# A fourth block pair in 11 products instead of 12, with the order of a pair's work searched anew

## The chip, the cores and the metric

The kernel runs on one core of a Trainium2 chip. The metric is the device time of one execution in microseconds (us). The engines are named as in the profile: PE multiplies matrices, DVE, ACT and POOL work on elements, SP issues most transfers.

## The reference

Input x has 8 sequences of 4096 tokens of 192 channels. A causal convolution of 7 taps (softmax weights, one set for each of 8 heads of 24 channels) is followed by an RMS norm and a gated layer with 1536 inner columns, all in float32:

```python
x_pad = np.concatenate([np.zeros((B, 6, D)), x], axis=1)        # 6 rows of zeros ahead of each sequence
y = np.einsum('hk,bskhg->bshg', w, windows_of_7(x_pad))          # w: softmax over the 7 taps
xn = y / np.sqrt(np.mean(y * y, axis=-1) + 1e-6) * rms_g
g, val = xn @ w_gate, xn @ w_val                                 # 192 -> 1536, twice
out = (g / (1 + np.exp(-g)) * val) @ w_out                       # 1536 -> 192
```

## The kernel before, in words

**Tiles.** The 32768 tokens are cut into 32 "pairs" of two tiles of 512 tokens. Pair 0 and pair 1 run in plain forms while the weights are prepared. Pairs 2 to 31, thirty of them, run the same program, and make nearly all of the time. The 1536 inner columns are cut into six "block pairs" j = 0 to 5 of 2 x 128 columns. A block pair has four cells: a, b, c, d, for two token tiles times two column blocks. A cell fills one two-bank PSUM tile (gate in one bank, value in the other), and there are four such tiles (`duo`). The upper 64 rows of PE work on the value, the lower 64 on the gate.

**Gate products.** The 192 input channels are three chunks of 64. In the plain form a cell is the sum of three products (letters A, B, E), 12 for a block pair. In the other form two of the chunks are multiplied as 2 x 2 blocks with seven products instead of eight (Strassen-Winograd), and the third chunk takes four: 11 products, P1 to P7 and Q1 to Q4. FORM says which block pair takes which form. A product is 6 matmuls (L898: three split parts, gate and value). In the 11-product form cells share sums, and this needs work on PSUM between products of one block pair:

- f1 copies cell a to b after P1 (ACT, L666), and P6 then adds into b;
- f3 copies cell c after P5 to SBUF (ACT at L666, or DVE at L668);
- f4 writes c = b + that copy (DVE, L969) after P6; P7 then adds into b;
- f5 writes d = b + that copy (DVE, L969) after P7, into the PSUM tile that cell a has given back; only then may the next product write on in b (Q3 or P4) or d (Q4).

When a cell is complete, `Ag` (ACT, L975) takes the silu of the gate, and `Vm` (DVE, L982) multiplies it by the value into `ht`; `Vm` gives the PSUM tile back. So a cell's tile is free for a later product only after silu and multiply.

**Output steps.** The output product uses seven products for 2 x 2 blocks too: seven forms o1 to o7 times six blocks, 42 steps of 6 small matmuls (L925; 12 records in the trace). Four "h" sums for each block (h1 to h4, DVE or POOL, L952) make their inputs. The three accumulators X, Y, Z sit in PSUM tiles; C22 and C21 (DVE, L999) and the copies c1, c2, s7 (ACT) collect them, and T11, T12, T21, T22 (DVE transposes, L940) turn them for the store (L1031).

**Token side.** For the next pair ahead: `cv0` to `cv6` are the convolution's taps (L432, L436), then square, reduce, `pow`, `bc`, `mul` make the norm; `pl` writes it to a scratch array and `ft` reads it back transposed (`xb`); x1 to x4 (L826) are the sums of token blocks for the 11-product form; n, l, d (L666, L812, L814) split the five operands into three float32r parts; `ld` loads the rows of x of the pair after that (`xh`).

**Order.** Every engine runs its instructions in the order in which they are issued. That order is written by hand or search in strings: LINE is the order of PE's 69 products and 42 steps of one pair; ORDER interleaves everything else with it. In ORDER, `p3` is the next three entries of LINE; a word's first letter is the engine (V DVE, A ACT, G POOL, S SP); `-` means the pair before, `+` the pair after. So `p5-` are five of the previous pair's output steps. FIRST is the same for pair 1, with W for the next step of the preparation of weight pieces. SP keeps a ring of ten weight pieces (192 KB each) filled: a piece's slot is loaded anew, in the order of first use, when its last product has been issued (`ring_load`, L784).

**Weight pieces.** `prepare` makes ten kinds of pieces (o = 0 to 9) for the block pairs that use them, splits them in three parts and writes them to the array `wd` (L748 to L767). `blocks` picks the block pairs: a slice with a constant step where the set has one, or else all six.

**Padding rows.** The first pair of each sequence has six rows of zeros ahead; `load_head` clears them in `xh` (L150).

Of the kernel before, what the change touches and what calls it, by code (L numbers as in the profile page):

```python
# [20 lines left out]
def kernel(  # L21
# [10 lines left out]
    nc = tc.nc  # L32
# [3 lines left out]
    H, K = weight.shape  # L36
    GS = D // H
# [9 lines left out]
    HALO = K - 1  # L47
# [20 lines left out]
    SPAN = 1509  # L68
    SPLIT = 2.0**-12
    HIGH = 0xFFFFF000  # L70
    FORM = (1, 0, 1, 0, 1, 0)
    PLAIN = tuple((j, c) for j in range(NP) for c in "abcd")
    ORDER = (
# [14 lines left out]
    )  # L88
    FIRST = (
# [12 lines left out]
    )  # L102
    LINE = (
# [7 lines left out]
    )  # L111

    cst = ctx.enter_context(tc.tile_pool(name="cst", bufs=1))
# [9 lines left out]
    x0 = cst.tile([P, NJ + HALO, D], F32, name="x0")  # L123
# [3 lines left out]
    def queue(eng):  # L127
        return nc.scalar if eng == "A" else nc.sync
# [8 lines left out]
    def load_head(p, b, t0, h, eng="S"):  # L137

        t = x_sb[p]

        def get(dst, tb, h, dims, r):
            row = x[b, t0 + tb * TB + r - HALO, h * GS :]
            src = bass.AP(
                tensor=row.tensor, offset=row.offset, ap=[dims, [D, TB + HALO - r], [1, GS]]
            )
            queue(eng).dma_start(out=dst, in_=src)  # L146

        first = int(t0 == 0)
        if first and h == 0:
            nc.gpsimd.memset(t[0:H, 0:HALO, :], 0.0)  # L150
            get(t[0:H, HALO:, :], 0, 0, [GS, H], HALO)
        get(t[first * H + h :: H], first, h, [TB * D, P // H - first], 0)

# [6 lines left out]
    def load(p):  # L160
# [34 lines left out]
        out=ps[6][:, 0 : H * K], lhsT=ones[:], rhs=w_row[:], start=True, stop=True,  # L195
# [24 lines left out]
    def load_in(u, q):  # L220
# [18 lines left out]
    nw = 4 * NP * (D // 2)  # L239
    tw = x0[:].rearrange("p j d -> p (j d)")[:, 0:nw].rearrange(  # L240
        "p (i k d) -> p i k d", i=4, k=NP
    )
    hs = work.tile([P, NP, T], F32, name="hs")
    tt = work.tile([P, 9, T], F32, name="tt")
    tiles = [tt[:, i, :] for i in range(few)]
# [2 lines left out]
    def load_out(i):  # L248
# [22 lines left out]
        out=taps[:], in0=w_sb, in1=stat[:].to_broadcast([P, H, K]), op=ALU.subtract  # L271
# [7 lines left out]
        out=taps[:], in0=taps[:], in1=ssum[:].to_broadcast([P, H, K]), op=ALU.mult  # L279
# [101 lines left out]
    def conv_first(mine, share):  # L381

        t = x_sb.pop(0)
        y = ys[0] = yp.tile([P, NJ, D], F32, name="y")
        theirs = [k for k in range(K) if k not in mine]
        two = NJ // 4
        for i, k in enumerate([theirs[0], mine[-1]] + theirs[1:]):
            xk, m = t[:, k : k + NJ, :], next(kept)
            cuts = (0, share) if k in mine else (0, H // 2, H)
            if k == theirs[-1]:  # L390
                cuts = (0, H // 2, H // 2 + 2, H)
            for lo, hi in zip(cuts, cuts[1:]):
                for h in range(lo, hi):
                    hs = slice(h * GS, (h + 1) * GS)
                    nc.scalar.mul(m[:, :, hs], xk[:, :, hs], taps[:, h, k : k + 1])
                part = slice(lo * GS, hi * GS)
                for c in range(4):
                    to = ps[c][:, 0 : two * D].rearrange("p (j d) -> p j d", d=D)
                    nc.tensor.matmul(
                        out=to[:, :, part], lhsT=unity, rhs=m[:, c * two : (c + 1) * two, part],  # L400
                        start=(i == 0 and lo == 0), stop=True, skip_group_check=True,
                    )
        for k in mine:
            xk = t[:, k : k + NJ, :]
            for h in range(share if k == mine[-1] else 0, H):
                hs = slice(h * GS, (h + 1) * GS)
                w = taps[:, h, k : k + 1]
                if k == mine[0]:
                    nc.vector.tensor_scalar(
                        out=y[:, :, hs], in0=xk[:, :, hs], scalar1=w, scalar2=None, op0=ALU.mult  # L410
                    )
                else:
                    nc.vector.scalar_tensor_tensor(
                        out=y[:, :, hs], in0=xk[:, :, hs], scalar=w, in1=y[:, :, hs],
                        op0=ALU.mult, op1=ALU.add,
                    )
        for c in range(4):
            at = y[:, c * two : (c + 1) * two, :].rearrange("p j d -> p (j d)")
            nc.vector.tensor_tensor(out=at, in0=ps[c][:, 0 : two * D], in1=at, op=ALU.add)
            if c % 2:  # L420
                heat(at, c)
# [296 lines left out]
    def blocks(o):  # L718

        kind = {2: 1, 4: 1, 6: 1, 8: 1, 9: 0}.get(o)  # L720
        mine = [j for j in range(NP) if kind in (None, FORM[j])]
        step = {b - a for a, b in zip(mine, mine[1:])}
# [419 lines left out]
    def done(it):  # L1142
# [21 lines left out]
        out=mask[:], in_=unity.rearrange("p (i h) -> p h i", h=H), axis=AX.X, op=ALU.add  # L1164
    )
    nc.vector.tensor_tensor(
        out=own[:], in0=taps[:].rearrange("p h k -> p k h"),
# [5 lines left out]
    load_out(1)  # L1173
    load_in(1, nc.sync)
    conv_first((1, 3, 5, 6), 2)
    nc.sync.dma_start(out=rg_sb[LOW, :], in_=rg)
    nc.sync.dma_start(out=rg_sb[UPP, 0 : KP - 1], in_=rg[:, 1:KP])
    nc.sync.dma_start(out=rg_sb[UPP, KP - 1 : KP], in_=rg[:, 0:1])
# [6 lines left out]
    p, sl, v = plain(first_hts)  # L1185
# [95 lines left out]
```

## Time and profile before

| what | us |
|---|---|
| three runs, median (range) | 2492.14 (2491.06 to 2493.56) |
| the profiled execution, its own time | 2491.27 |
| its span (first to last instruction) | 2489.5 |
| PE busy | 2475.4 |
| DVE busy | 2014.9 |
| ACT busy | 926.5 |
| POOL busy | 847.1 |
| matmuls at L898 (gate products) | 12420 |
| matmul records at L925 (output steps) | 16200 |

The granted PE clock is full speed from end to end. The transfer queue that carries all the kernel's own data is busy for 63.6% of the 16 engines' span. One line of the timeline view has the start, the duration, the engine, the source line and operation, output and inputs, shapes and the count of instructions merged in it; in brackets stands the idle time before it, and what ended that.

### The profile page before, as it was taken

The page shows a single profiled execution, that of the slowest core. Times are in us where ns is not written, and L with a number is a line of the kernel's source. Part 1 is how long each engine was busy: PE and PEld are TensorE (multiplying, and loading weights), DVE is VectorE, ACT ScalarE, POOL GpSimd, SP SyncE. Part 2 cuts the span into 40 slices and gives each one's busy share as a digit, 9 for nine tenths or more (in the row PEclk, how much of TensorE's full clock was granted, in tenths as well). Part 3 has the DMA queues.
Part 4 walks back from the last instruction along what each step waited for, and adds up shares of the span by engine and source line. Part 5 has one row for each costly group of instructions (what it writes and reads, how often), then busy time and mean ns, then how long its engine had stood idle before and what let it go on. Part 6 is the DMA issues. An engine that isn't in the chain of part 4 may idle for free.

```text
span 2489.5 us, 69349 instructions
## 1 busy us (share of the span) xinstructions
PE 2475.4 (99%) x29332; PEld 1971.8 (79%) x29332; DVE 2014.9 (81%) x2492; ACT 926.5 (37%) x1345; POOL 847.1 (34%) x634
## 2 busy tenths in 40 slices
PE   8999999999999999999999999999999999999999
PEld 5547778888788887888887788887888788888787
DVE  8678878888878788878788787888787888888874
ACT  6443333333334333334333343333333333333331
POOL 0542333323343324243333333233433243433331
PEclk9999999999999999999999999999999999999999
DMA  7365667766667666667666677666676666776652
GB/s 150 60 197 152 162 160 190 182 176 157 157 171 201 172 168 159 161 176 200 170 158 156 166 194 178 177 157 157 171 205 170 164 161 157 183 196 174 152 148 80
DMA packets 702935, 412.23 MB, mean 166 GB/s; under 512 B 508834, under 2 KB 688930, under 8 KB 702626
## 3 DMA queue, kind: packets, MB, share of 16 engines
q1 hardware_dynamic: 698880, 406.89, 63.6%
q8 instruction: 231, 3.78, 0.7%
q10 hardware_dynamic: 3746, 0.92, 0.2%
q14 instruction: 78, 0.64, 0.1%
HBM read 349.26 MB, written 58.39 MB: 164 GB/s over the span
## 4 chain that ended last, share of the span: by engine, by line
PE 95%; DMA 2%; DVE 1%; SPq 1%; issue 1%; POOL 0%; ACT 0%; DVEq 0%; POOLq 0%; ACTq 0%
PE ps L898 57%; PE ps L925 36%; PE ps L870 2%; DMA xb<-xd 1%; DVE ht L1097 0%; SPq L146 0%; SPq L230 0%; DVE y L436 0%; DMA hs<-in_moe_w_out_dram 0%; DMA x<-in_x_dram 0%; DMA ht<-in_moe_w_gate_dram 0%; DMA ht<-in_moe_w_val_dram 0%; DVE part L336 0%; POOL part L327 0%; DVE part L321 0%
## 5 line engine op out<-in xcount | busy, mean ns | idle before, releaser
L898 PE MATMUL ps<-part,ring 64*128 64x512 f32 x12420 | 1443.4, 389 | 0.0
L898 PEld LDWEIGHTS ps<-part,ring 64*128 64x128 f32 x12420 | 1234.7, 184 | 188.1 <-issue 18.3
L975 ACT ACTIVATE tt<-ps 128x512 f32<-128x512 f32 x744 | 431.8, 598 | 759.4 <-PE ps L898 719.7
L982 DVE TENSOR_TENSOR ht<-ps,tt 128x512 f32<-128x512 f32 x744 | 495.8, 685 | 190.0 <-ACT tt L975 184.9
L925 PE MATMUL ps<-ht,wo_sb 128*32 128x384 f32 (+2 forms) x7272 | 474.7, 380 | 1.9 <-DVE ht L982 1.0
L925 PE MATMUL ps<-ht,x 128*32 128x256 f32 (+2 forms) x6696 | 441.9, 379 | 0.0
L952 POOL TENSOR_TENSOR ht<-ht 128x512 f32<-128x512 f32 x183 | 280.0, 1544 | 431.3 <-PE ps L925 377.2
L925 PEld LDWEIGHTS ps<-ht,wo_sb 128*32 128x32 f32 x7272 | 320.1, 110 | 128.7 <-issue 23.1
L952 POOL TENSOR_TENSOR hs<-ht 128x512 f32<-128x512 f32 x90 | 116.4, 1294 | 835.9 <-DVE ht L982 833.6
L925 PEld LDWEIGHTS ps<-ht,x 128*32 128x32 f32 x6696 | 302.5, 110 | 90.7
L436 DVE SCALAR_TENSOR_TENSOR y<-xh,tp,y 128x1536 f32<-128x1536 f32 x186 | 342.8, 1843 | 1.3
L666 ACT COPY ps<-ps 128x384 f32<-128x384 f32 (+1 forms) x121 | 104.1, 860 | 409.6 <-PE ps L898 312.9
L969 DVE TENSOR_TENSOR ps<-ps,tt 128x1024 f32<-128x1024 f32 x180 | 221.3, 1229 | 42.6 <-PE ps L898 35.6
L666 ACT COPY tt<-ps 128x384 f32<-128x384 f32 (+1 forms) x122 | 90.9, 745 | 227.1 <-PE ps L925 207.9
L925 PE MATMUL ps<-hs,x 128*32 128x128 f32 (+2 forms) x2232 | 161.0, 379 | 0.0
L925 PEld LDWEIGHTS ps<-hs,x 128*32 128x32 f32 x2232 | 108.8, 110 | 27.8
L952 DVE TENSOR_TENSOR ht<-ht 128x512 f32<-128x512 f32 x189 | 127.4, 688 | 3.4 <-PE ps L925 3.3
L666 ACT CAST part<-xb 128x1024 fp32r<-128x1024 f32 x87 | 91.4, 1050 | 89.5 <-PE ps L898 75.9
L952 DVE TENSOR_TENSOR ht<-hs,ht 128x512 f32<-128x512 f32 x155 | 121.2, 798 | 2.9 <-PE ps L925 1.1
L952 DVE TENSOR_TENSOR hs<-ht 128x512 f32<-128x512 f32 x96 | 121.8, 1269 | 2.1
L814 DVE SCALAR_TENSOR_TENSOR part<-part,xb 128x1024 fp32r<-128x1024 f32 x87 | 106.2, 1221 | 0.0
L812 DVE TENSOR_TENSOR part<-xb,part 128x1024 fp32r<-128x1024 f32 x87 | 105.5, 1213 | 0.0
(132 smaller groups left out, 1389.7 us busy)
## 6 DMA issues: line engine op xcount, KB each, us to landing
ring<-wd SPq DMA_DIRECT2D x1350, 192.0 KB
xb<-xd SPq DMA_DIRECT2D x60, 512.0 KB
xd<-xh SPq DMA_DIRECT2D x240, 96.0 KB
xh<-in_x_dram SPq DMA_DIRECT2D x192, 105.0 KB
xb<-xd SPq DMA_DIRECT2D x60, 256.0 KB
out_dram<-o_sb SPq DMA_DIRECT2D x126, 96.0 KB
out_dram<-o_sb SPq DMA_DIRECT2D x62, 128.0 KB
wd<-part SPq DMA_DIRECT2D x5, 1152.0 KB
```

Source lines behind the costliest of these rows:

```text
L436: nc.vector.scalar_tensor_tensor(out=y, in0=xk, scalar=w, in1=y, op0=ALU.mult, op1=ALU.add)
L666: nc.scalar.copy(out=dst, in_=src)
L812: e.tensor_tensor(out=split_of(g, 1).bitcast(F32R), in0=src, in1=high, op=ALU.subtract)
L814: nc.vector.scalar_tensor_tensor(out=split_of(g, 2).bitcast(F32R), in0=high, scalar=1.0 + SPLIT, in1=src, op0=ALU.mult, op1=ALU.subtract,)
L870: nc.tensor.matmul(out=self.both(j, c)[:, h, :], lhsT=wf[HALF[h], k, 2 * j + f, :], rhs=rb[HALF[h], k, g, :], start=(k == 0), stop=(k == K ...
L898: nc.tensor.matmul(out=self.both(j, c)[:, h, :], lhsT=left[HALF[h]], rhs=right[HALF[h]], start=(first and q == 0), stop=True, skip_group_c ...
L925: nc.tensor.matmul(out=self.acc(b)[i * Q : (i + 1) * Q, at : at + n], lhsT=left, rhs=cols, start=fresh, stop=True, skip_group_check=True, ...
L952: engine[eng].tensor_tensor(out=dst, in0=a, in1=b, op=op)
L969: nc.vector.tensor_tensor(out=self.both(j, c), in0=self.both(j, "b"), in1=s5, op=ALU.add)
L975: nc.scalar.activation(out=tt[:, t, :], in_=self.both(j, c)[:, 0, :], func=AF.Silu)
L982: nc.vector.tensor_tensor(out=self.hv(j, "abcd".index(c)), in0=self.both(j, c)[:, 1, :], in1=tt[:, t, :], op=ALU.mult,)
```

## The change

FORM becomes (0, 1, 1, 0, 1, 1): block pairs 1, 2, 4, 5 in 11 products (block pairs 0, 2, 4 before), so LINE has 68 products and 42 steps. ORDER, FIRST and LINE are other sequences. With four block pairs 1, 2, 4, 5 there is no constant step, so `blocks` returns all six for the pieces 2, 4, 6, 8 (three before), and two (0 and 3) for piece 9. In ORDER the token sums x1 to x4 and the splits l are all on DVE (POOL had x2, x3, x4 and one l), and the four f1 are on ACT, three f3 on ACT and one on DVE. In `load_head` the zeros come by a transfer from a small tile that POOL clears once, instead of a POOL memset each time.

```diff
-    FORM = (1, 0, 1, 0, 1, 0)
+    FORM = (0, 1, 1, 0, 1, 1)
...
     ORDER = (
...
-        "p8- Gh4.4- Gh4.1- VT11- VC22- p2- p1 Gl.4 Acv0+ Af1.0 VT22- VC21- p1- VT21- p3 Vcv1+",
-        "p1 Af3.0 Sst1.2- Vcv2+ Vf4.0 p3- p3 Aga.0 Sst1.0- Vcv3+ VT12- Vma.0 Sst0.2- Agc.0",
...
+        "Ac1- An.3 p13- An.2 As7- An.4 Vd.3 Ac2- Acv0+ p12- Gh4.2- Vh4.3- Vl.0 Vh4.4- Vl.2",
+        "Vd.2 Vd.0 Vl.3 Vl.1 Vl.4 Vd.4 Vd.1 VC22- Gh4.0- Vh4.1- VT11- Vcv1+ Vh4.5- p8- VC21-",
+        "p1 Vcv2+ VT12- p11 Agd.0 Vcv3+ Vcv4+ VT22- Agc.0 Vmd.0 Vcv5+ Vmc.0 Aga.0 p1 Vma.0 p2",
+        "Agb.3 Vmb.3 VT21- Af1.1 Vcv6+ p5 Af3.1 Agb.0 Vf4.1 p1 Vmb.0 Aga.1 Vma.1 p3 Asq+",
+        "Vf5.1 Vred+ p3 Agd.1 Agc.1 p1 Aga.3 Vmd.1 Vmc.1 Gpow+ p1 Af1.2 p1 Agb.1 Vma.3 p4",
+        "Vbc+ Vmb.1 Af3.2 Aga.2 Gmul+ p1 Sst1.3- Spl.0+ Vf4.2 Vma.2 p3 Spl.1+ Agc.2 Vf5.2",
...
     LINE = (
-        "P1.0 P5.0 P6.0 P2.0 Q1.0 P7.0 P3.0 Q2.0 Ac.1 Q4.0 Q3.0 P4.0 Bc.1 Ec.1 Aa.1 Ba.1 Ea.1",
...
+        "Ad.0 Bd.0 Ed.0 Aa.0 Ab.3 Ea.0 Ac.0 Ec.0 Bc.0 Bb.3 Ba.0 Eb.3 P1.1 Ab.0 P5.1 Eb.0 P6.1",
+        "Bb.0 Q1.1 P2.1 P7.1 Q2.1 P3.1 Aa.3 Q4.1 Ea.3 Ba.3 P4.1 P1.2 Q3.1 P5.2 P6.2 P2.2 Q1.2",
+        "Ac.3 P7.2 P3.2 Q2.2 Q3.2 P4.2 Q4.2 P1.4 Ec.3 Bc.3 P5.4 P6.4 P2.4 Ad.3 Q1.4 P7.4 Q2.4",
+        "P3.4 Bd.3 Ed.3 Q4.4 P1.5 Q3.4 P5.5 P4.4 P2.5 P6.5 Q1.5 o1.0 o1.2 o1.4 P7.5 P3.5 Q2.5",
+        "P4.5 Q4.5 Q3.5 o1.3 o7.0 o1.1 o1.5 o7.1 o7.3 o2.3 o2.4 o2.0 o7.2 o7.5 o6.0 o7.4 o6.5",
+        "o6.1 o2.5 o6.3 o6.2 o6.4 o4.4 o2.1 o5.5 o4.0 o5.2 o5.4 o5.0 o5.1 o4.5 o2.2 o5.3 o4.3",
+        "o4.1 o4.2 o3.3 o3.4 o3.2 o3.1 o3.0 o3.5",
     )
...
-            nc.gpsimd.memset(t[0:H, 0:HALO, :], 0.0)
+            queue(eng).dma_start(out=t[0:H, 0:HALO, :], in_=zeros)
...
+    zeros = x0[:].rearrange("p j d -> p (j d)")[0:H, nw : nw + HALO * GS]
...
+    nc.gpsimd.memset(zeros, 0.0)
```

48 rows, old and new, of tables (FIRST, LINE, ORDER) are left out of this document.

## The prediction

> **What bounds the kernel now.** I read the page's shares first, then its chain, then the waits, and last the timeline of one token block ("pair") in the steady state.
>
> ```profile
> PE 2475.4 (99%) x29332; PEld 1971.8 (79%) x29332; DVE 2014.9 (81%) x2492; ACT 926.5 (37%) x1345; POOL 847.1 (34%) x634
> PE 95%; DMA 2%; DVE 1%; SPq 1%; issue 1%; POOL 0%; ACT 0%; DVEq 0%; POOLq 0%; ACTq 0%
> PEld ps L925 <- DVE ht L982: 12.0, 30, 1.1
> PEld ps L898 <- DVE ht L982: 5.9, 29, 0.2
> POOL xh L150 <- DMA ring<-wd: 82.6, 7, 12.3
> ```
>
> PE is busy all the time and makes 95% of the chain. Its waits for others are tens of microseconds in 2489.5, so time is lost only by adding PE work or by making PE wait. POOL's long wait for the padding rows (L150) is on nobody's path.
>
> The unit of account is one pair. By the start times in the trace, 28 steady pairs follow each other every 75.67 us. Inside, a gate product (6 matmuls at L898) takes 0.680 from start to start, an output step (12 records at L925) 0.645.
>
> ```profile
> 999.78 19.96 PE L898 MATMUL ps<-part,ring 64*128 64x512 f32 x174
> 1044.51 0.96 PE L898 MATMUL ps<-part,ring 64*128 64x512 f32 x6
> 1045.40 0.86 PE L925 MATMUL ps<-ht,wo_sb 128*32 128x384 f32 x12
> 1046.19 3.01 PE L898 MATMUL ps<-part,ring 64*128 64x512 f32 x24
> 1049.13 2.16 PE L925 MATMUL ps<-ht,wo_sb 128*32 128x384 f32 x36
> 1051.22 5.17 PE L898 MATMUL ps<-part,ring 64*128 64x512 f32 x41
> ```
>
> The first row: 29 products in 19.96, 0.688 with the drain at the end. The others: PE changes between products and steps. From 1044.51 to 1045.40 one product takes 0.89, to 1046.19 one step 0.79, to 1049.13 four products 2.94: each change of kind costs 0.10 to 0.14, and the first product after it 0.13 more, 0.39 a round trip. So a pair before: 69 x 0.680 + 42 x 0.645 = 74.01, three round trips 1.17, steps that take 0.650 late in the phase 0.10: 75.28. The other 0.39 of the 75.67 are small waits, the largest 0.12 and 0.06.
>
> **What the change removes.** One product per pair (block pair 2 had 12, now 11): -0.68. In the new order the last 33 steps of the pair before come in one piece, so PE changes kind and back twice, not three times: -0.39. A pair in which PE never waited would take 68 x 0.680 + 42 x 0.645 + 0.78 + 0.10 = 74.21, 1.46 less than now, 44 us in 30 pairs. That is what there is to win.
>
> **What it adds, and what hides it.** Per pair DVE gets two adds of L969 (2 x 1.23), three token sums from POOL (0.69 each alone) and one split (1.21), and gives one block sum away on balance (-1.27 - 0.80 + 0.68): 4.4 us more on about 65. ACT gets two copies (1.00 and 1.02) on about 29. Three more weight pieces come through the ring (48 for 45, 192 KB each). By the order of the products a piece is still asked for 7 or more products (4.8 us) before its use, as before, and the transfers' share has room (63.6%): 0, with three ring waits below 0.5 us as the upper end. The padding rows' 7 small transfers of 8 x 576 bytes take SP some 0.6 us each, and SP waits 856.6 us for PE in all: 0 either way.
>
> In the output phase DVE must do, from the start of the last multiply to the first collection of results: that multiply 0.60, three sums 2.0, seven block sums 4.3, ten splits at 1.14 from start to start, 11.4: 18.3. PE gives it 30 steps x 0.645 + 0.1 + 0.40 until the collection may start, less 0.8 until the multiply may: 19.05. Cost 0, with 0.75 us to spare; what runs over it costs 30 us for each us.
>
> **The new waits.** Delays from the trace: PE's end to the start on ACT or DVE 0.23 (0.40 after an output step); the end on DVE or ACT to PE 0.18 (the four places where PE was held by it give 0.15 to 0.21).
>
> ```profile
> 1003.39 0.60 ACT L975 ACTIVATE tt<-ps 128x512 f32<-128x512 f32 x1 [0.37 <-PE ps L898]
> 1004.02 0.69 DVE L982 TENSOR_TENSOR ht<-ps,tt 128x512 f32<-128x512 f32 x1
> 1004.63 1.22 DVE L969 TENSOR_TENSOR ps<-ps,tt 128x1024 f32<-128x1024 f32 x1
> ```
>
> These three make the chain that an 11-product block needs: cell a complete, silu, multiply (which frees its bank), the second add into that bank, and only then the products that write on in b and d. With its delays: 0.23 + 0.60 + 0.03 + 0.69 + 0.10 + 1.23 + 0.18 = 3.06. The add also needs P7: 0.23 + 1.23 + 0.18 = 1.64 from P7's end. The new LINE gives it:
> - block 1, P2.1 to Q4.1: four products, 2.72: PE waits 0.34
> - block 2, Q1.2 to Q3.2: four, 2.72: 0.34
> - block 4, Q1.4 to Q4.4: five, 3.40, with Vh1.2 in between on DVE (3.47): 0.07
> - block 5, P7.5 to P4.5: two, 1.36 of 1.64: 0.28
>
> Together 1.03. Before, the same chain of block 4 had six products and that of block 0 three output steps and four products; only Q4.0 lost 0.06.
>
> The second place is the start of a pair, where DVE runs without a gap from the collection VC22 on (0.40 after the last step of form 5). From start to start: C 0.59, h 0.60, T 0.57, cv 1.73, h 0.60, C 0.59, cv 1.73, T 0.57, cv 1.85, cv 1.73, T 0.57, m 0.60, cv 1.73. POOL's two sums h4.2 and h4.0 begin about 0.3 before that last step ends, take 1.29 each, and the second still holds DVE's first cv for about 0.45, as the rows below show such holds. So Vmc.0 starts 14.3 after that step, and its end reaches PE at 15.18. Ab.0 would start at nine steps + change + 13 products, 14.92: late 0.26. Then Vma.0, Vmb.3, the copy Af1.1 (1.00): P6.1 is late by another 0.20. Four smaller ones by the same sums: P1.2 0.08, P6.2 0.04, P7.2 0.05, P2.5 0.04.
>
> ```profile
> 1010.04 1.30 POOL L952 TENSOR_TENSOR hs<-ht 128x512 f32<-128x512 f32 x1 [14.16 <-DVE ht L982]
> 1011.42 1.29 POOL L952 TENSOR_TENSOR ht<-ht 128x512 f32<-128x512 f32 x1
> 1011.55 1.71 DVE L952 TENSOR_TENSOR hs<-ht 128x512 f32<-128x512 f32 x1
> ```
>
> DVE's sum, 0.69 alone, takes 1.71: it ends 0.55 after POOL's. The bounds of this hold: nothing (alone), or POOL's whole 1.29.
>
> **Sum.** New waits 1.03 + 0.46 + 0.21 = 1.70 against 1.46 won: +0.24 a pair, +7.2 us in 30. Once: at the end T22 and T21 now stand behind T12, so ACT's six stores (5.38 us) come after the last step, not three: +2.7. In pair 1 four of the ten weight pieces are prepared for six blocks instead of three; DVE already waits 8.0 us there for the writes of the full ones, and would wait as much again, but has 14.5 us free in those 62, and PE's banks lie several us ahead: between 0 and 10, I take 1, near the row of before in which such waits cost PE nothing. Total +10.9. The profiled execution took 2491.27 (span 2489.5 and 1.8 around it); the median of the runs is 0.87 above it. 2492.14 + 10.9 = **2503 us**, 0.4% slower. A measurement of this kernel can tell about 0.2% (5 us) from no change.
>
> **Rivals.**
> 1. The forecast: the won product is given back to banks that come free too late. For it: each chain is summed from rows, and PE cannot pass a waiting product. 2494 to 2512. Chance 0.58.
> 2. The hold of DVE by POOL at the start is small, so the 0.46 there goes: 75.45 a pair, 6.6 less than before, with the once-only 3.7: 2489. For it: POOL may be released a little earlier. Chance 0.17.
> 3. Also the small waits and half of the four chains are hidden: 75.91 - 0.46 - 0.21 - 0.5 = 74.74, -28 + 3.7: 2468; with only the first two, 2483. For it: 44 us are there to win, and no wait of before is over 0.12. Against: the chains leave no slack to hide them. Chance 0.15.
> 4. POOL takes the port first: h4.0 gets in ahead of DVE's Vh4.1, which then ends 1.27 later. By its last step (needs Vh4.5) PE is held 0.86 a pair: +26 us, 2529. It decides if POOL's second sum is issued before DVE's. Against: in the trace a waiting DVE sum went ahead of POOL's next. The same price comes from an output phase that overruns its 0.75 by as much. Chance 0.10.
>
> The Trainium skill (SBUF — State Buffer, "Who interferes with whom") says of rival 4's port that a DVE instruction with two SBUF inputs and a GpSimd one that reads SBUF exclude each other for a whole instruction, and that the order of issue decides. The 1.71 above agrees; it speaks against this change, which puts two such GpSimd sums beside the one stretch where DVE has no slack, and would make the time rival 4's if GpSimd were first.
>
> That the change does not do what it says is excluded for the products: the built program has 12,240 matmuls at that line for 12,420.
>
> **Numbers.** The range takes rivals 1 and 2 and the near part of 3: 2483 to 2514, with about 0.18 outside. Faster: rival 3, 0.15. Same: rival 2 and the low end of 1, 0.22. Slower: 0.63.
>
> **What would show it.** PE's page row would fall below 99% of the span, or its L898 starts show gaps at Q4.1, Q3.2 and P4.5 of 0.3 each; steady pairs 75.9 apart; DVE near 70 us of a pair; no L150 on POOL. Pairs of 75.0 or less would refute the chains; pairs over 76.3 mean DVE is late in the output phase or held by POOL.

## The result, and the profile after

The changed kernel takes 2521.78 us (median of four runs, 2519.95 to 2524.9) against 2491.6 for the kernel before: 1.0123 times, 95% interval 1.0105 to 1.014. It is slower, as forecast, but by 30 us instead of 11, and outside the range of 2483 to 2514.

The shares of the page after, then the longest waits of PE and of its weight loads (what waits on what; us in total, times, longest):

```profile
PE 2479.5 (98%) x29152; PEld 1919.2 (76%) x29152; DVE 2102.1 (83%) x2642; ACT 999.8 (40%) x1405; POOL 653.5 (26%) x538
PE 92%; DVE 2%; DMA 1%; SPq 1%; issue 1%; POOL 1%; ACT 1%; DVEq 0%; POOLq 0%; ACTq 0%
```

```profile
PE ps L926 <- DVE ht L953: 12.0, 1, 12.0
PE ps L871 <- DVE ht L983: 7.2, 6, 2.2
...
PEld ps L899 <- DVE ps L970: 24.3, 60, 0.5
```

PE has 180 gate matmuls fewer, but its busy time is not less, its share falls from 99% to 98%, and the chain runs 8% of the span outside it, not 5%. Two of these lines are new and happen outside the thirty equal pairs: one wait of 12.0 us at an output step, and six, 7.2 together, at L871 (line 870 before), which makes pair 1's products. The third is the wait for f5 that the prediction priced, 60 times: in each of the 30 pairs once at Q3.2 and once at P4.5. The two others that it priced, at Q4.1 and Q4.4, the profile books as "issue".

By the starts of PE's instructions in the two traces (us):

| stretch | before | after | difference |
|---|---|---|---|
| up to pair 1's first product | 124.9 | 124.8 | -0.1 |
| pair 1's products | 62.0 | 70.9 | +8.9 |
| pair 1's output steps | 24.8, and four steps (2.6) inside pair 2 | 40.3 | +12.8 |
| pair 2, start to start | 75.6 | 78.0 | +2.4 |
| the next 28 pairs, mean | 75.670 | 75.756 | +2.4 in all |
| the last pair (before: less those 2.6) | 75.6 | 75.8 | +0.2 |
| from the last matmul to the end | 5.2 | 7.3 | +2.1 |
| span | 2489.5 | 2518.1 | +28.6 |

So 24 of the 29 us are lost once, in pair 1 and just behind it. The profiled execution is the lowest of the four runs.

**The clock behind the wait.** The page's row of the granted PE clock after the change (one digit for each fortieth of the span, in tenths of full speed):

```profile
PEclk9998999999999999999999999999999999999999
```

The 8 comes from 13.7 us, from 227.1 to 240.7, in which the granted clock was 0.50. They begin inside the 12.0 us wait and reach into pair 2. Pair 1's last step takes 1.44 us for 0.86, and pair 2's first four products take 1.44, 1.28, 1.28 and 1.09 for 0.82, 0.69, 0.70 and 0.69 in later pairs. That is 2.8 us, and 2.2 of them are nearly all of pair 2's 2.4. In the kernel before the clock was halved only behind the last matmul.

**The 12 us wait.** SP's issues at the end of pair 1, after the change (SPq is SP's sequencer):

```profile
184.82 4.07 SPq L146 DMA_DIRECT2D xh<-in_x_dram  x4
217.27 5.72 SPq L785 DMA_DIRECT2D ring<-wd  x10
223.03 4.41 SPq L146 DMA_DIRECT2D xh<-in_x_dram  x4
```

Half of the loads of pair 3's x go out at 184.8. Then SP stands until 217.3 at the first ring load, whose memory still holds pair 2's tokens (a split on DVE reads them last); only behind the ten ring loads do the other four x loads go out. In FIRST, `R` stood behind all eight x loads before, and stands ahead of the last four now. SP in the kernel before:

```profile
179.22 7.43 SPq L146 DMA_DIRECT2D xh<-in_x_dram  x8
204.86 11.24 SPq L784 DMA_DIRECT2D ring<-wd  x14
```

PE's wait after the change ends by a chain: x loads, ACT's first tap of pair 3, DVE's next tap, and only then DVE's sum h4.5 for pair 1's last step, which stands behind that tap in ORDER.

```profile
ACT y L433 <- DMA xh<-in_x_dram: 106.4, 21, 19.7
DVE y L437 <- ACT y L433: 12.5, 1, 12.5
```

### The profile page after: what moved, and what is told of

It is laid out like the page before. It is cut to its first block, busy times and chain, and to the rows that moved or that the text cites. A ratio compares the mean times of both kernels' runs of the same rounds, so it can differ in the third digit from the quotient of the medians.

```text
span 2518.1 us, 69213 instructions
## 1 busy us (share of the span) xinstructions
PE 2479.5 (98%) x29152; PEld 1919.2 (76%) x29152; DVE 2102.1 (83%) x2642; ACT 999.8 (40%) x1405; POOL 653.5 (26%) x538
## 4 chain that ended last, share of the span: by engine, by line
PE 92%; DVE 2%; DMA 1%; SPq 1%; issue 1%; POOL 1%; ACT 1%; DVEq 0%; POOLq 0%; ACTq 0%
PE ps L899 57%; PE ps L926 34%; PE ps L871 1%; DMA wd<-part 1%; SPq L230 0%; SPq L146 0%; POOL part L762 0%; DVE y L437 0%; DVE ht L1098 0%; DMA hs<-in_moe_w_out_dram 0%; DVE part L758 0%; DVE part L815 0%; DVE part L813 0%; DMA x<-in_x_dram 0%; DMA ht<-in_moe_w_gate_dram 0%
## 5 line engine op out<-in xcount | busy, mean ns | idle before, releaser
L899 PEld LDWEIGHTS ps<-part,ring 64*128 64x128 f32 x12240 | 1174.2, 184 | 264.2 <-issue 34.7
L926 PE MATMUL ps<-ht,wo_sb 128*32 128x384 f32 (+2 forms) x7272 | 458.2, 380 | 12.8 <-DVE ht L953 12.0
L953 POOL TENSOR_TENSOR ht<-ht 128x512 f32<-128x512 f32 x152 | 209.2, 1386 | 898.9 <-PE ps L926 565.3
L926 PE MATMUL ps<-ht,x 128*32 128x384 f32 (+2 forms) x6696 | 419.5, 379 | 0.0
L437 DVE SCALAR_TENSOR_TENSOR y<-xh,tp,y 128x1536 f32<-128x1536 f32 x186 | 349.2, 1877 | 13.7 <-ACT y L433 12.5
L970 DVE TENSOR_TENSOR ps<-ps,tt 128x1024 f32<-128x1024 f32 x240 | 295.6, 1232 | 57.7 <-PE ps L899 29.5
L667 ACT COPY tt<-ps 128x1024 f32<-128x1024 f32 (+1 forms) x152 | 121.6, 800 | 151.3 <-PE ps L926 148.9
L667 ACT COPY ps<-ps 128x1024 f32<-128x1024 f32 (+1 forms) x151 | 134.0, 887 | 85.3 <-DVE ht L983 40.1
L953 DVE TENSOR_TENSOR ht<-ht 128x512 f32<-128x512 f32 x220 | 167.1, 760 | 0.1
L926 PE MATMUL ps<-hs,x 128*32 128x384 f32 (+2 forms) x2232 | 149.3, 379 | 0.0
L953 POOL TENSOR_TENSOR ht<-hs,ht 128x512 f32<-128x512 f32 x62 | 80.6, 1300 | 93.9 <-DVE ht L953 62.9
L433 ACT ACTIVATE y<-xh,tp 128x1536 f32<-128x1536 f32 x29 | 45.8, 1579 | 145.9 <-DMA xh<-in_x_dram 106.4
```

What stands on the lines that cost most here:

```text
L433: nc.scalar.mul(y, xk, w)
L437: nc.vector.scalar_tensor_tensor(out=y, in0=xk, scalar=w, in1=y, op0=ALU.mult, op1=ALU.add)
L667: nc.scalar.copy(out=dst, in_=src)
L899: nc.tensor.matmul(out=self.both(j, c)[:, h, :], lhsT=left[HALF[h]], rhs=right[HALF[h]], start=(first and q == 0), stop=True, skip_group_c ...
L926: nc.tensor.matmul(out=self.acc(b)[i * Q : (i + 1) * Q, at : at + n], lhsT=left, rhs=cols, start=fresh, stop=True, skip_group_check=True, ...
L953: engine[eng].tensor_tensor(out=dst, in0=a, in1=b, op=op)
```

## Experiments

Each time is a median. The ratio behind it, with its 95% interval, is to the kernel before on the same chip (2489.8 to 2491.0 us there). The kernel before took 2491.6 beside the changed kernel; as it differs by up to 1.8 us from one such comparison to another, a difference of one or two us between two versions says little.

### The order of the loads

**e1**: only the loads are moved back.

```diff
-        "... Vh2.5 p1 R",
-        "Sld.4++ Sld.5++ Sld.6++ Sld.7++",
+        "... Vh2.5 p1",
+        "Sld.4++ Sld.5++ Sld.6++ Sld.7++ R",
```

> After the change, with the loads of rows 4 to 7 of pair 3's x put back ahead of the ten first weight loads in FIRST, and nothing else. Theory (29 us are nearly all lost once, in pair 1: some 15 of them because these four loads stand on SP behind ring loads that may only start when the ring's memory is free): 12 to 15 us less than the changed kernel, 2507 to 2510; the 12.0 us wait of PE for a DVE sum at the end of pair 1 is gone. Rival (pair 1's output steps are late because the preparation of weights pushed DVE's work into them): 0 to 3 us less, 2519 to 2522, the wait stays.

Measured: 2509.24, 12.5 us less than the changed kernel, 1.0074 (1.0059 to 1.0089). The wait is gone, pair 1's output steps take 27.5 us for 40.3, pair 2 76.0 for 78.0, and the clock is not halved there. These stretches give 14.8; 1.9 are lost ahead of them, as pair 1's products take 72.8 us for 70.9. That is the clock again: behind a wait of 2.2 us that both kernels have at this place, it was halved in e1 for 3.4 us (180.8 to 184.3) and not in the changed kernel, and two cells took 2.12 and 2.22 us for 1.36 and 1.29. SP in e1:

```profile
185.11 7.78 SPq L146 DMA_DIRECT2D xh<-in_x_dram  x8
219.25 5.89 SPq L785 DMA_DIRECT2D ring<-wd  x10
```

The ring loads are not earlier than after the change; only the x loads no longer stand behind them. The rival falls.

**b1**: the same exchange in the kernel before, in the other direction.

```diff
-... Sld.4++ Vmc.5 p2 Sld.5++ ... Sld.6++ ... Sld.7++ ... p2 R p7 As7 p7
+... Vmc.5 p2 ... p2 R Sld.4++ Sld.5++ Sld.6++ Sld.7++ p7 As7 p7
```

> The kernel before, with the loads of rows 4 to 7 of pair 3's x moved behind the ten first weight loads in FIRST, as the change has them, and nothing else. Theory (the place of these loads alone costs): 6 to 14 us slower than before, 2497 to 2505, all of it at the start of pair 2's products or just ahead of them, where ACT's and DVE's taps of pair 3 hold the silus behind them; later pairs are as before. Rival (it costs only in the new order, where DVE has no slack in the output steps): within 2 us of before.

Measured: 2499.03, 8.5 us slower than before, 1.0029 (1.0018 to 1.0041). Pair 2 takes 84.8 us for 75.6, the other pairs 75.62. PE waits once for 6.1 us, and from within this wait on the clock is halved for 10.2 us, which costs some 3 more. The order of these loads costs in either kernel.

**e7**: the order of the text stays as the change has it; another engine issues.

```diff
-        "Sld.4++ Sld.5++ Sld.6++ Sld.7++",
+        "Ald.4++ Ald.5++ Ald.6++ Ald.7++",
```

> After the change, with the four late loads of x (rows 4 to 7 of pair 3) issued by ACT instead of SP, at the same place of FIRST's text, behind the ring loads, and nothing else. Theory (these loads are late because SP, which issues in order, stands at ring loads that wait for memory; the transfers themselves are not in each other's way): most of e1's gain, 9 to 13 us less than the changed kernel, 2508 to 2513, and PE's 12.0 us wait at the end of pair 1 gone. Rival (another issuing engine only saves the time of issuing, as the Trainium skill's page DMA: Bandwidth & Descriptors, section Issuing engines are not separate DMA queues, has it): at most the 5.7 us that SP takes to issue the ten ring loads, 2516 to 2522.

Measured: 2508.56, 13.2 us less than the changed kernel, 1.0077 (1.006 to 1.0094), as much as e1. ACT issues the four loads between 197.6 and 200.8, SP the ring loads from 219.0 on. So what made the loads late was SP's program order: issued by ACT they are out before the ring loads start. Pair 1's products take 72.8 us here too, with the clock halved from 179.9 to 183.3.

The rule of the Trainium skill (DMA: Bandwidth & Descriptors, "Issuing engines are not separate DMA queues"), that another issuing engine saves only the time of issuing, does not cover an issue that stands at a wait: the ten issues took 5.7 us, and 13.2 were won.

### The preparation of the pieces

**e2**: block pairs 3, 4, 5 are renamed 5, 3, 4, so that those of 11 products have a constant step.

```diff
-    FORM = (0, 1, 1, 0, 1, 1)
+    FORM = (0, 1, 1, 1, 1, 0)
...   (in LINE, ORDER and FIRST's h2: 3 is written 5, 4 is 3, 5 is 4)
```

> After the change, with the block pairs renumbered (3 becomes 5, 4 becomes 3, 5 becomes 4), so that those of 11 products are 1 to 4 and weight pieces 2, 4, 6, 8 are prepared for four block pairs instead of all six, piece 9 for 0 and 5. The order of the work is the same. Theory (some 9 us are lost in pair 1's products to preparing three block pairs too many in each of these pieces): two thirds of it comes back, 3 to 7 us less than the changed kernel, 2515 to 2519; pair 1's products take 63 to 67 us for 70.4, and the 12 us wait at its end stays. Rival (the products of pair 1 are late because DVE and POOL do the preparation in another order, whatever its size): 0 to 1.5 us less.

Measured: 2517.71, 4.1 less than the changed kernel, 1.0108 (1.0091 to 1.0125). Pair 1's products take 66.6 us for 70.9.

**e3**: e1 and e2 together.

> Both edits: the loads ahead of the ring loads, and pieces for four block pairs. Theory (two separate losses): the gains add, 15 to 22 us less than the changed kernel, 2500 to 2507, still 8 to 15 slower than before. Rival (one cause with two faces): hardly more than the larger of the two alone. Steady pairs unchanged at 75.76 for either.

Measured: 2503.75, 18.0 less, 1.0054 (1.0039 to 1.0069). The gains add (12.5 and 4.1, and 1.4 more; e3 is without the halved clock that cost e1 1.7). Two losses, then, and 13 us to before are left, 4.6 of them still in pair 1's products.

**b2**: in the kernel before, six block pairs instead of three.

```diff
+        if o in (2, 4, 6, 8):
+            return slice(0, NP)
```

> The kernel before, with weight pieces 2, 4, 6, 8 prepared for all six block pairs instead of three, and nothing else. Theory (three block pairs too many in four pieces make the wait in pair 1's products): 6 to 10 us slower than before, 2497 to 2501, pair 1's products take 68 to 72 us for 62.0. Rival (the order of preparation steps in the new FIRST makes it): 0 to 2 us slower.

Measured: 2495.63, 5.1 slower than before, 1.0018 (1.0009 to 1.0027); products 66.5 us for 62.0. The size is half of the 8.9; theory and rival each had half.

**s6**: e3 with FIRST of the kernel before. In it the sums h2 of pair 1 stand ahead of output steps that should read the values they replace, so pair 1's output is not the reference's; the work is the same.

> Both edits of e3, and FIRST's order of the preparation steps, token work and loads as in the kernel before (without the five words that the new ORDER holds). Theory A (size alone: pieces for four block pairs instead of three): pair 1's products still 65 to 67 us, 2502 to 2505. Theory B (half of what is left in pair 1 is FIRST's order): products 62 to 64 us, 3 to 4 us less than e3, 2499 to 2501.

Measured: 2503.19, pair 1's products 62.0 as theory B has it, but its output steps 30.0 for 28.9, and the steady pairs 75.88 on the mean for e3's 75.81, so that the whole time is theory A's.

**f1**: the same with FIRST's own last part, h2 included.

```diff
     FIRST = (
-        "... Vmc.0 W p1 Gpow+ W W W p1 W W p1 Agd.0 Vmd.0 ... Gmul+ W p1 W Aga.1",
+        "... Vmc.0 W p1 Gpow+ W W W p1 W p1 Agd.0 W Vmd.0 ... Gmul+ p1 Aga.1 Vh3.0 W",
...   (the steps W where the kernel before has them, up to the last product)
```

> e3 with FIRST's preparation steps placed as in the kernel before up to the last product, and the rest of FIRST as the change has it, loads ahead of the ring. Theory (s6: the place of the preparation steps, not only their size, costs half of pair 1's loss): pair 1's products 62 to 63 us, output steps 28 to 29, 4 to 5 us less than e3: 2498.5 to 2500. Rival (what the products win, the output steps lose, as DVE's work of the preparation comes later): 0 to 2 us less than e3.

Measured: 2500.29, 3.5 less than e3, 1.0036 (1.0022 to 1.0049). Products take 62.0 and output steps 28.9, as the theory has them; the steady pairs, 75.87 on the mean for 75.81, take back some of what pair 1 wins. PE's row for pair 1's products (busy us, mean ns; idle us and what ended it) in the kernel before, after the change, in b2 and in f1:

```profile
L870 PE MATMUL ps<-xb,part 64*128 64x512 f32 x288 | 62.1, 590 | 0.0
```

```profile
L871 PE MATMUL ps<-xb,part 64*128 64x512 f32 x288 | 63.8, 595 | 7.2 <-DVE ht L983 7.2
```

```profile
L872 PE MATMUL ps<-xb,part 64*128 64x512 f32 x288 | 63.4, 593 | 2.7 <-DVE ht L984 2.7
```

```profile
L871 PE MATMUL ps<-xb,part 64*128 64x512 f32 x288 | 62.1, 590 | 0.0
```

f1 has the row of before: four block pairs cost nothing if the steps W stand where the kernel before has them. They cost 4.6 where the change puts them, and two more block pairs 4.3 on top. In both rows that wait, PE waits for a multiply that frees a bank. After the change DVE itself waits in this stretch, 5.3 us for writes to `wd`, 4.8 for ACT's and 2.9 for POOL's part of the same steps, and the multiplies stand behind. The kernel before and f1 wait for these writes longer, 8.0 and 8.4 us, and PE loses nothing: what counts is which multiply stands behind such a wait.

### The padding rows

**e4**: the memset is put back.

```diff
-            queue(eng).dma_start(out=t[0:H, 0:HALO, :], in_=zeros)
+            nc.gpsimd.memset(t[0:H, 0:HALO, :], 0.0)
```

> After the change, with the padding rows cleared by POOL's memset again. Theory and prediction: within 1 us of the changed kernel; POOL's wait of some 12 us at each of the seven sequences' starts is back, and nobody waits for POOL. Rival (the seven small transfers hold SP or the loads behind them): 2 us or more less.

Measured: 2543.62, 22 us slower than the changed kernel, 1.0211 (1.0196 to 1.0226). Both expectations fail. Every fourth pair, the one in which a sequence's first rows are loaded, is 1.7 to 4.4 us longer. In three of the seven the clock was halved for 3.4 us behind PE's wait; these are 4.0 to 4.4 longer, the four others 1.7 to 2.3. POOL there, and PE's waits:

```profile
1200.63 0.21 POOL L150 MEMSET xh<- 8x144 f32 x1 [15.70 <-DMA xd<-xh]
1200.81 1.28 POOL L953 TENSOR_TENSOR ht<-ht 128x512 f32<-128x512 f32 x1
```

```profile
PE ps L926 <- DVE ht L983: 15.0, 8, 2.6
```

POOL stands 15.7 us at the memset, for the scratch writes that still read the tile, and its sums h stand behind. They then run beside DVE's sums, and DVE's take 1.8 us where they take 0.68 without POOL beside them:

```profile
1208.13 1.77 DVE L827 TENSOR_TENSOR tt<-xb 128x512 f32<-128x512 f32 x1
1209.82 1.76 DVE L953 TENSOR_TENSOR ht<-ht 128x512 f32<-128x512 f32 x1
1211.50 1.87 DVE L983 TENSOR_TENSOR ht<-ps,tt 128x512 f32<-128x512 f32 x3
```

The third row begins with the multiply that PE waits for. In the kernel before POOL waited up to 12.3 us at the same place, but in its ORDER seven products lie between the loads and POOL's next sum, h1.3. In the new one POOL's h3.2 stands right behind `Sld.0++`, and that does no harm only because SP takes the zeros.

### The steady pairs

PE's waits in the steady pairs come where the prediction put them. DVE, ACT and weight loads ahead of Q4.1, after the change:

```profile
1009.84 0.60 ACT L976 ACTIVATE tt<-ps 128x512 f32<-128x512 f32 x1 [0.78 <-PE ps L899]
...
1010.48 0.69 DVE L983 TENSOR_TENSOR ht<-ps,tt 128x512 f32<-128x512 f32 x1 [0.69 <-ACT tt L976]
1011.27 1.23 DVE L970 TENSOR_TENSOR ps<-ps,tt 128x1024 f32<-128x1024 f32 x1
1012.41 1.74 DVE L459 TENSOR_REDUCE s<-xh 128x64 f32<-128x1536 f32 x1
1012.62 1.25 PEld L899 LDWEIGHTS ps<-part,ring 64*128 64x128 f32 x12 [0.52 <-issue]
```

Silu, multiply, second add f5, and 0.12 after its end the weight loads of Q4.1 go on. The profile books this wait as "issue", but the semaphore that ends it is f5's.

**s5**: a filler ahead of the two products that wait most (on top of e3, so 3, 4, 5 are its names).

```diff
-... P3.1 Aa.5 Q4.1 Ea.5 Ba.5 ... Q2.2 Q3.2 P4.2 Q4.2 P1.3 Ec.5 Bc.5
+... P3.1 Aa.5 Ea.5 Q4.1 Ba.5 ... Q2.2 Ec.5 Q3.2 P4.2 Q4.2 P1.3 Bc.5
-... Agd.1 Agc.1 p1 Aga.5 Vmd.1 Vmc.1 ... Vh1.2 Vf5.3 Vmc.3
+... Agc.1 Agd.1 p1 Aga.5 Vmc.1 Vmd.1 ... Vf5.3 Vmc.3 Vh1.2
```

> Both edits of e3, and in LINE one product of a plain block pair moved ahead of Q4.1 and of Q3.2, with the silu and multiply of cell c of block pair 1 ahead of those of d; and DVE's h1.2 behind f5 of the third block pair. Theory (PE waits for f5's chain at these places, 0.38, 0.32 and 0.11 us a pair with the drain, and another 0.10 at P2 after it): the waits go, 0.5 to 0.9 us a pair, steady pairs 74.9 to 75.25 us apart for 75.77, 2477 to 2488 us, faster than before. Rival (a bank that comes late at one place comes late at the next, so the wait only moves): steady pairs 75.6 or more, 2499 to 2504.

Measured: 2502.28, 1.0043 (1.0028 to 1.0058), 1.5 less than e3 and so not clearly less; steady pairs 75.73 (median; 75.77 in e3). The rival is right:

```profile
PEld ps L899 <- DVE ht L983: 31.8, 62, 0.5
...
PEld ps L899 <- DVE ps L970: 11.2, 30, 0.4
```

Of 60 waits for f5 30 are left, and 62 for the multiply have come. Q4.1 and Q3.2 no longer wait; P1.2 and P5.3 do, for the bank that a multiply frees. For P1.2 DVE shows why: the norm's reductions (L459 and the two behind it) stand ahead of that multiply.

```profile
994.39 1.74 DVE L459 TENSOR_REDUCE s<-xh 128x64 f32<-128x1536 f32 x1
...
996.59 1.88 DVE L983 TENSOR_TENSOR ht<-ps,tt 128x512 f32<-128x512 f32 x3
```

**v1**: s5 without the move of Ec.5, and the reductions in two parts.

```diff
-Asq+ Vf5.1 Vred+ ... Vmc.1 Vmd.1 Gpow+ ... Vma.5 p4 Vbc+ Vmb.1 ... Gmul+ p1 Sst1.3- Spl.0+ Vf4.2 Vma.2
+Asq+ Vf5.1 ... Vmc.1 Vre1+ Vmd.1 ... Vma.5 Vre2+ Gpow+ p4 Vmb.1 ... p1 Sst1.3- Vf4.2 Vma.2 Vbc+ Gmul+
...   (the scratch writes pl up to eight products later)
```

> e3 with Q4.1 behind Ea.5 and the silu and multiply of c ahead of those of d (as in s5, without s5's move of Ec.5), h1.2 behind f5, and DVE's three reductions of the norm out of the way: the long one between the multiplies of c and d, the two short ones behind that of Aa.5; pow, bc, mul and the scratch writes move back with them. Theory 1 (in s5 the wait only moved from Q4.1 to P1.2 because the reductions, 2.3 us, held DVE's multiply of c, which frees P1.2's bank): the 0.38 us of Q4.1 are won, steady pairs 75.2 to 75.45, 2489 to 2496. Theory 2 (four PSUM tiles are too few for this form, whatever DVE does): the wait turns up again within the next six products, steady pairs 75.6 to 75.75, 2499 to 2503.

Measured: 2502.87 (2498.7 to 2509.5), no better than e3. The profiled execution is the slowest of the five. In it 8 of the 28 steady pairs take 75.2 to 75.45 us, as theory 1 has it, and in these no wait comes in place of Q4.1's within six products; but the other 20 are longer, one of them 80.2 with a wait of 2.8 us and the clock halved behind it, and the mean is 76.03.

**v2**: v1 with f1's FIRST and, in the last pair, C21 and both turns of token block 2 earlier.

```diff
+        if w == PAIRS:
+            words = " ".join(words).replace("p8- VC21-", "VT22- p2- VC21- VT21- p6-").split()
```

> v1 with FIRST of f1, and in the last pair C21, T22 and T21 ahead of the last six output steps. Theory: the three gains add (pair 1 minus 4.5, the end minus 2, steady pairs as in v1): 2482 to 2490, faster than before by 0.1 to 0.4%; from the last matmul to the end of the span 5.2 us for 7.2. Rival (theory 2 of v1): 2493 to 2497, slower than before.

Measured: 2496.2, 1.0021 (1.0012 to 1.003): the fastest version with the new forms, and still slower than before, as the rival had it. The end takes 5.4 us for 7.2. Twelve of the 28 steady pairs take 75.2 to 75.4, and the mean is 75.81. DVE's x sums now wait for the transposed reads, which they hardly did after the change (0.4 us in all):

```profile
DVE tt L834 <- DMA xb<-xd: 10.9, 12, 3.0
```

**v3** and **v4** bring mul and the writes forward (v4 two reads too), with x3 later on DVE.

```diff
-... Vf4.2 Vma.2 Vbc+ Gmul+ ... p2 Spl.0+ p1 Spl.1+ ... Vma.3 Spl.7+ Agc.3 ... p1 Vx3+ Vh3.3 ... Vmb.4 Vx1+
+... Vf4.2 Vbc+ Gmul+ Vma.2 ... Spl.0+ p1 Spl.1+ p1 Spl.2+ ... p2 Spl.7+ Vf4.3 ... p1 Vh3.3 ... Vmb.4 Vx3+ Vx1+
```

> v2 with bc and mul directly behind f4 of the third product form's block pair 2, the eight scratch writes each one to four products earlier, and DVE's x3 two steps later. Theory (in v2 every second pair loses 0.3 to 4 us because the transposed reads come late and DVE's x sums and ACT's splits wait for them ahead of work that PE needs): these pairs come back to the clean ones of v2, 75.2 to 75.35, mean over all below 75.45, 2481 to 2487, faster than before. Rival (what is lost there is lost to four PSUM tiles and the transfers' own spread): mean 75.7 or more, 2492 to 2497.

> v3 with the first two transposed reads also two products earlier. Theory (the reads are late): as v3 or up to 3 us less, 2479 to 2486. Rival (SP waits at the reads for the writes, and the weight loads behind it come late): PE waits for ring transfers, slower than v3 by 2 us or more.

Measured: 2520.44 and 2525.89. Neither gain comes: v3 is far outside its theory and its rival, v4 is as its rival has it. In v3 PE waits for the ring in 20 of the 30 pairs, at P2.4 and P6.4:

```profile
PE ps L906 <- DMA ring<-wd: 15.9, 22, 1.2
```

SP issues in order: writes brought together ahead of the weight loads make those late. These waits are 15.9 us (2.0 in v2) of the 24 us between v2 and v3; the rest stays open.

**v6** leaves the writes where v2 has them, **v7** changes only x3's place.

> v2 with bc and mul directly behind f4 of block pair 2 and x3 two steps later; the scratch writes stay where v2 has them. Theory (in v3 the writes, brought together, came ahead of ring loads that PE then waited for; the late x sums are the rest): no ring waits at P6.4 and Q1.4, fewer late pairs than v2, mean 75.4 to 75.7, 2485 to 2494. Rival (any order of these writes costs ring loads or late reads): 2494 or more.

> v2 with only x3 two steps later. Theory: of v2's loss in late pairs, the part at the output steps (6.4 us in the profiled execution) goes, the part at the products (2.7) stays: 2488 to 2492. Rival (the output steps wait for the reads at the next DVE or ACT step instead): 2494 to 2498.

Measured: 2502.57 and 2501.93, steady pairs 75.98 and 75.99 on the mean. The ring waits go from 15.9 to 2.5 us in v6, but both are slower than v2: v6 is within its rival's "2494 or more", v7 outside theory and rival. In v7 nothing but x3 moved: 0.7 us of DVE's work from a place with room into the output phase. DVE's x sums hardly wait for the reads any more (1.1 us for 10.9), and yet three places lose: the last step o3.4 comes 0.2 us later, for a sum of DVE, Ab.0 loses 0.07, and P6.1 0.09 more than in v2 (medians). Even the shortest pair takes 75.40 us for v2's 75.21. So the 0.75 us to spare that the prediction counted there are not all free.

## Why the prediction was right in its sign and wrong in its size

Two steps of the prediction failed, both in what happens once: the price of pair 1's preparation, and the place of the x loads, which had no term at all. The second is the larger, and it alone takes the forecast out of its range (2503 + 15.2 = 2518); the first alone would have left it inside (2511).

- **The once-only cost of pair 1**, "between 0 and 10, I take 1", was 8.9 in the profile. The reason given, that DVE had 14.5 us free and PE's banks lay ahead, is about sums of time; DVE runs in order, and a multiply behind a waiting step of the preparation is late however much time is free. Half was the size (b2, e2), half the new places of the steps in FIRST (f1), which the prediction did not price at all.
- **The order of R and the x loads** was not a term, and no reason was given for leaving it out. The change shows it in FIRST's last two lines. It cost 12.8 us at pair 1's end and 2.4 in pair 2 (e1, e7, b1): 12.0 of waiting, and 2.8 at the halved clock that followed. That a weight piece is asked for 7 or more products before its use says when a piece is needed, not what stands behind a ring load in SP's queue. With these two terms at their measured 24 in place of 1, the forecast of 2503 would have been 2526, and with the steady pairs and the tail as measured about 2521.
- **The f5 chains**, 1.03 a pair: right, place by place. The medians of PE's loss, with the slow first product after the wait: Q4.1 0.38, Q3.2 0.32, Q4.4 0.11, P4.5 0.24, together 1.05.
- **The start of a pair**, 0.46: over-sized, about 0.08 was seen, all at P6.1. The hold was there:

```profile
1217.41 0.56 DVE L1000 TENSOR_TENSOR tt<-ps,tt 128x384 f32<-128x384 f32 x1 [0.64 <-PE ps L926]
1217.88 0.75 DVE L953 TENSOR_TENSOR ht<-ht 128x512 f32<-128x512 f32 x1
...
1219.12 2.27 DVE L437 SCALAR_TENSOR_TENSOR y<-xh,tp,y 128x1536 f32<-128x1536 f32 x1
...
1231.06 1.88 DVE L983 TENSOR_TENSOR ht<-ps,tt 128x512 f32<-128x512 f32 x3
```

  The first tap takes 2.27 us, later ones 1.80. But a collection C passes on after 0.47 from start to start, not 0.59, twice, and the multiply of c starts 13.65 after the first C, where the sum had 13.9. Ab.0 is then just in time, at the 14.92 it needs. Where the sum had Ab.0 late by 0.26 there is no loss, but no margin either.
- **The four small waits**, 0.21: P2.5 0.10, P6.2 0.06, P1.2 and P7.2 0.01 each, 0.18.
- **The steady pair**, +0.24: +0.086, of the forecast's sign; in the 28 pairs 2.4 us for 6.7. The named places lose 1.31 of the 1.46 to be won, not 1.70, and alone would have made the pair 0.15 faster. The other 0.24 are small losses and changes of kind that no term had, none of them much over 0.1, as the kernel before has 0.39 of small waits. So the mechanism, rival 1, is right for the most part, and the sign of the pair is in part luck. v1 and v2 show that the banks are not the last word: with DVE's reductions out of the way the shortest pairs are 0.5 us shorter, below the kernel before. So something of rival 3 was there to be had, but no order tried here has it in all pairs.
- **The tail**, +2.7: +2.1, and v2's end gives 1.8 of it back.
- **Covered at nothing**: the output phase (no step of it waits after the change) and the ring (no wait of PE for it) were right. The transfer of the zeros costs nothing, as forecast; that it is worth 22 us in the new order was not seen.
- **Rival 4** did not come: DVE's waiting sum goes ahead of POOL's second, as before. That the time lies nearer to its 2529 than to the forecast is chance. The Trainium skill's rule of the shared port (SBUF — State Buffer, "Who interferes with whom") agrees with the held tap, 2.27 for 1.80; PE lost at most the 0.08 of P6.1 by it.

Left open: why the clock was halved behind the 2.2 us wait in pair 1's products in e1 and e7 and not behind the same wait after the change and in e4; and whether some order of the token side gives every pair v2's 75.2.

## What to carry to other kernels

A steady loop that is priced to a tenth of a microsecond can still be the small part: read the code that runs once, line by line, and ask for every queue what stands behind an instruction that waits. Free time on an in-order engine hides nothing that stands behind a wait. And where a wait is taken away, look which instruction holds the next bank before counting the gain.

## What was not expected of the hardware

- A transfer's issue that waits holds every later issue of that engine: ACT waited 19.7 us for four loads of 105 KB behind ten ring loads, and with ACT as their issuer the kernel won 13.2 us (e7). A POOL memset of 0.21 us that waited 15.7 was followed by waits of PE of up to 2.6 us (e4).
- Beside long waits of PE the granted clock was halved: for 13.7 us with the 12.0 us wait, for 10.2 with b1's 6.1, for 3.4 with e1's and e7's 2.2. In such a stretch a product took 1.28 us for 0.68, so that the wait was not all that it cost.
- A wait of PE costs more than itself: the product after it takes 0.09 to 0.12 longer too (Q4.1 0.77, Q3.2 and P4.5 0.80 for 0.68).
